# Loading the FFTs' half-way rows: one transfer over 128 partitions, two over 64

## The chip, the cores and the metric

The kernel runs on one core of a Trainium2 chip. The metric is the device time of one execution in microseconds, and lower is better. Before the change, three runs gave 878.99, 880.49 and 887.65 us, a median of 880.49.

A core has TensorE (PE, matrix products; PEld is its loading of weights), VectorE (DVE), ScalarE (ACT), GpSimd (POOL) and SyncE (SP). SP, ACT and POOL can issue DMA transfers, which run on the core's 16 DMA engines. On-chip memory has 128 partitions; DRAM holds inputs, outputs and scratch tensors.

## The reference

One forward pass and its gradients, with L = 2048 positions, D = 448 channels, N = 256 states and F = 1792 hidden units, all in bf16:

```python
g = sigmoid((x * gate_w).sum(-1, keepdims=True))
# branch A: a state-space convolution, computed by FFT
P = exp(dt * A * l)                      # l = 0..2047, rounded to bf16
K = einsum("dn,dnl,dn->dl", C, P, dt * B).real
a = irfft(rfft(pad(u)) * rfft(pad(K)))[:L] + u * Dskip
# branch B: two dense layers with a squared relu
b = relu(x_B @ w1 + b1) ** 2 @ w2 + b2
out = g * a + (1 - g) * b
# returned: out, and the gradients of all inputs but x_B for a given grad_out
```

The gradient of the convolution needs two more products in the frequency domain: one that gives the gradient of K, and one that gives the gradient of u.

## The kernel before

**FFTs in two steps.** A transform of 2048 positions, padded, is done as a product with one small matrix, a trip through DRAM that reorders the rows, and a product with a second small matrix. The forward trips go through the scratch tensors gd[0..2], the inverse ones through hd[0..2]. An inverse transform's first half (inv1_part at L304, or inv1 at L275) writes hd in eight stores of 448 KB, each as 128 x 4 rows of 896 bytes (L315, L291). Its second half reads hd in four quarters q. A quarter is a tile of 128 partitions by 3,584 elements: partitions 0 to 63 take the 64 rows that begin at row 8q of each group of 64 rows in hd, partitions 64 to 127 the rows that begin at 32 + 8q. So a partition receives one contiguous run of 8 x 448 elements, 7,168 bytes, and the two halves differ by a shift of 32 rows. load_hs (L317) does this, with two DMAs on SP's queue.

**Three readers of hd.**
- hd[0] is the convolution that gives the gradient of the taps K. load_taps (L693) issues all four quarters at once into the tile hss, after the last of the eight stores. dk_sums (L701) multiplies them by the Ew matrices on TensorE (L712), copies the sums out on ScalarE (L716), writes them to dk_d (L725) and reads them back as DK (L730).
- hd[1] is the convolution's forward output. A loop over q (L1640) reads one quarter with inv2 (L322, TensorE at L329) and finishes it on VectorE (L1653, L1654). The load for the next quarter is issued while the loop works on this one (L1657).
- hd[2] is the gradient of u. A second loop (L1683) reads one quarter per turn; the first load stands ahead of the loop (L1681), the others one turn ahead (L1686). Its output is copied out at L1697 and stored by four DMAs on SP at L1704.

hd[1] and hd[2] quarters and the spectra that load_sx reads from sp_d (L1556, 896 KB) share a ring of three buffers.

**What sets the order.** Engines execute their instructions in the order of the program. From L562 that order is written out by hand. In the last part, Fl(n) puts n units of other work (the dense layers' weight gradients, L1217 to L1257) between the steps, and Pg(n) puts pieces of the parameters' gradients on VectorE (L1479 to L1526). SP's queue there carries, in program order: the hd stores (L291), sp loads (L1556), hd loads (L320), br loads (L1587, 448 KB), the parameter loads for the last two groups of channels (L1445, L1459, L1460), whose buffer L1674 frees, and the output stores (L1704). POOL's queue carries rows_in (L1212) and stores of outputs. A wait that stands before a DMA on SP holds everything behind it on SP.

**Around the taps.** After the load of the taps SP issues the next rec tile (L629) and w1 (L1170, L1172), which VectorE needs at L786 and TensorE at L995. powers (L580) is a chain between ScalarE (L610, L613) and VectorE (L611, L615) that runs in pieces beside it.

Of the kernel before, what the change touches and what calls it, by code (L numbers as in the profile page):

```python
# [20 lines left out]
L, D, N, F = 2048, 448, 256, 1792  # L21
# [144 lines left out]
class Ker:  # L166
# [148 lines left out]
            queue.dma_start(bass.AP(tensor=hd, offset=4 * q8 * 128 * D, ap=[[D, 128], [128 * D, 4], [1, D]]), st)  # L315

    def load_hs(self, hd, q, hs):  # L317
        for hp in range(2):
            src = bass.AP(tensor=hd, offset=(32 * hp + 8 * q) * D, ap=[[64 * D, 64], [1, 8 * D]])
            self.nc.sync.dma_start(hs[64 * hp:64 * hp + 64].rearrange("p g x d -> p (g x d)"), src)  # L320

    def inv2(self, hs, q, x, hp, ps, more=()):  # L322

# [11 lines left out]
def kernel(ctx, tc, A_u, A_A_re, A_A_im, A_B_re, A_B_im, A_C_re, A_C_im, A_log_dt, A_Dskip,  # L335
# [1286 lines left out]
    Fl(3)  # L1622
    back1(0, 3)
    hsn = load_hs(1, 0)
    Fl(2)
    product(1, 1, sx[1])
# [13 lines left out]
    for q in range(4):  # L1640
# [15 lines left out]
        if q < 3:  # L1656
            hsn = load_hs(1, q + 1)  # L1657
# [21 lines left out]
    obs += [Dw[:, 6144:7680], GU_[:, 10240:11776]]  # L1679
    pgs = (None for dt in range(2, 4) for _ in param_grads(dt))  # L1680
    hsn = load_hs(2, 0)  # L1681
    Fl(8)
    for q in range(4):  # L1683
# [75 lines left out]
```

## Time and profile before

| | |
|---|---|
| median of three runs | 880.49 us |
| the profiled execution | 872.19 us |
| its span, first to last instruction | 870.4 us |
| mean granted TensorE clock | 0.885 |
| busy: PE, DVE, ACT, POOL | 75%, 78%, 66%, 21% of the span |
| DMA packets, bytes | 138,036, 181.16 MB |
| DMA, mean share of the 16 engines, 140 to 190 us | 0.82 |
| the same, 734 to 816 us and 816 to 870 us | 0.81 and 0.56 |
| granted clock, 140 to 190 us and 734 to 816 us | 0.68 and 0.92 |

The profile is of one execution. Times in its views count from the start of the span. A busy engine is not one that sets the end: what does is read from the chain of waits, which goes back from the last instruction, at each step to what released it. A DMA's time in that chain runs from its issue to its landing, when its last byte is known to be in place and the semaphore that readers wait for is full. The shares of the DMA engines are averages over the 16; a stretch in which two of them work all the time and 14 rest shows as 0.125.

The trace also lists each DMA packet (queue, size, start, duration) and each update of a semaphore by a DMA, with its time. The packets do not carry the name of their engine.

### The profile page before, as it was taken

What the parts mean: (1) busy time and instruction counts of PE and PEld (TensorE: products, weight loads), DVE (VectorE), ACT (ScalarE), POOL (GpSimd) and SP (SyncE); (2) the same over time, 40 slices, a digit from 0 to 9 for tenths busy, and PEclk for the clock granted to TensorE, in tenths of its full rate; (3) what the DMA queues carried; (4) which work ended last, traced back from release to release, by engine and by line L of the source; (5) the groups of instructions that cost most, each with busy time, mean ns of one, the idle gap of its engine ahead of it and who ended that gap; (6) DMA issues with size and microseconds to landing.
All of it is one profiled execution on the core that took longest, in us unless ns stands there. A gap on an engine that the chain in (4) does not pass through costs nothing.

```text
span 870.4 us, 19323 instructions
## 1 busy us (share of the span) xinstructions
PE 654.3 (75%) x7849; PEld 344.6 (40%) x7849; DVE 676.5 (78%) x1124; ACT 578.4 (66%) x845; POOL 179.7 (21%) x297
## 2 busy tenths in 40 slices
PE   3857662567688788998978897987847884888496
PEld 2213221342434545554554454455524342444242
DVE  4686998774997888999999989998447965775166
ACT  1896753678787989997858675767734772544262
POOL 1443102141112000000202120214433310123012
PEclk9965797858699889999989987999979997999699
DMA  9968798951555953877456657394889999796872
GB/s 193 265 188 311 232 397 290 251 184 73 156 167 188 229 126 104 189 192 192 133 153 156 206 147 190 97 224 122 202 286 341 290 307 316 247 287 207 237 188 62
DMA packets 138036, 181.16 MB, mean 208 GB/s; under 512 B 67511, under 2 KB 111532, under 8 KB 137420
## 3 DMA queue, kind: packets, MB, share of 16 engines
q1 hardware_dynamic: 116156, 105.94, 45.6%
q0 software_dynamic: 21360, 72.09, 24.9%
q10 hardware_dynamic: 432, 1.90, 1.0%
q8 instruction: 61, 1.00, 0.5%
q14 instruction: 27, 0.22, 0.1%
HBM read 96.97 MB, written 68.97 MB: 191 GB/s over the span
## 4 chain that ended last, share of the span: by engine, by line
PE 31%; ACT 17%; issue 16%; DVE 15%; DMA 14%; POOL 3%; SPq 3%; ACTq 0%; POOLq 0%; DVEq 0%
PE psX L1230 7%; PE psN L1022 4%; PE psN L995 3%; DVE D L665 2%; DVE Y L770 2%; DMA K<-hd 2%; DVE F L771 2%; DMA gd<-R 2%; DMA K<-gd 2%; PE psF L903 1%; PE psF L863 1%; ACT R L865 1%; DVE P L919 1%; DVE Y L773 1%; DMA hd<-st 1%
## 5 line engine op out<-in xcount | busy, mean ns | idle before, releaser
L1022 PE MATMUL psN<-D,S 128*128 128x448 bf16 x448 | 97.0, 365 | 0.0
L773 DVE TENSOR_TENSOR Y<-Y,F 128x256 bf16<-128x256 bf16 (+2 forms) x84 | 72.8, 867 | 2.9
L770 DVE TENSOR_TENSOR Y<-Y,F 128x256 bf16<-128x256 bf16 (+2 forms) x84 | 72.8, 867 | 2.7
L771 DVE TENSOR_TENSOR F<-Y,F 128x256 bf16<-128x256 bf16 (+2 forms) x84 | 71.8, 855 | 0.0
L908 ACT CAST R<-psF 128x1024 bf16<-128x1024 f32 x56 | 57.1, 1019 | 10.2 <-PE psF L903 8.9
L995 PE MATMUL psN<-S,U 128*128 128x512 bf16 x168 | 49.0, 420 | 16.4 <-ACT S L984 11.2
L1230 PEld LDWEIGHTS <-S 128*128 128x128 bf16 x448 | 43.3, 102 | 44.6 <-issue 15.1
L919 DVE TENSOR_TENSOR P<-R 128x2048 bf16<-128x2048 bf16 x42 | 49.4, 1220 | 13.7 <-ACT R L908 13.7
L1022 PEld LDWEIGHTS <-S 128*128 128x128 bf16 x448 | 41.9, 101 | 42.7 <-issue 11.6
L1230 PE MATMUL psX<-D,S 128*128 128x449 bf16 x224 | 51.9, 379 | 1.9 <-ACT S L1237 1.9
L1027 POOL DMA_DIRECT2D br_d<-D x32 | 17.5, 547 | 169.0 <-ACT D L1026 169.0
L822 PE MATMUL psX<-X,Y 128*64 128x16 bf16 x1792 | 39.1, 185 | 15.2 <-DVE Y L773 15.2
L1126 PE MATMUL psN<-S,U 128*128 128x512 bf16 x168 | 44.1, 395 | 5.5 <-ACT S L1135 5.5
L863 PE MATMUL psF<-ident,Y 128*128 128x128 bf16 x448 | 34.4, 238 | 15.8 <-ACT R L865 13.3
L1221 ACT ACTIVATE S<-psN 128x1024 bf16<-128x1024 bf16 x33 | 33.8, 1025 | 18.0 <-PE psN L1217 18.0
L822 PEld LDWEIGHTS <-Y 128*64 128x64 bf16 x1792 | 37.4, 125 | 19.7 <-DVE Y L773 16.5
L865 ACT COPY R<-psF 128x2048 bf16<-128x2048 bf16 x15 | 28.0, 1866 | 22.4 <-PE psF L863 22.4
L759 DVE TENSOR_TENSOR X<-X,F 128x512 bf16<-128x512 bf16 (+1 forms) x70 | 37.5, 536 | 2.6
L1105 POOL DMA_DIRECT2D dhT_d<-S x28 | 20.3, 727 | 89.4 <-DVE S L1102 60.7
L1230 PE MATMUL psX<-U,S 128*128 128x448 bf16 x176 | 37.7, 358 | 1.1 <-ACT S L1234 1.1
L863 PEld LDWEIGHTS <-Y 128*128 128x128 bf16 x448 | 30.2, 107 | 19.5 <-issue 15.7
L760 DVE TENSOR_TENSOR F<-X,F 128x512 bf16<-128x512 bf16 (+1 forms) x70 | 36.9, 528 | 0.0
(330 smaller groups left out, 1660.1 us busy)
## 6 DMA issues: line engine op xcount, KB each, us to landing
hd<-st SPq DMA_DIRECT2D x19, 448.0 KB, 4.0
sp<-K POOLq DMA_DIRECT2D x8, 896.0 KB, 8.6
S<-rT_d SPq DMA_DIRECT2D x16, 448.0 KB, 5.7
dhT_d<-S POOLq DMA_DIRECT2D x28, 256.0 KB, 3.3
S<-rT_d POOLq DMA_DIRECT2D x14, 512.0 KB, 6.4
R<-sp SPq DMA_DIRECT2D x8, 896.0 KB, 10.1
S<-dhT_d POOLq DMA_DIRECT2D x14, 512.0 KB, 5.6
R<-hd SPq DMA_DIRECT2D x16, 448.0 KB, 8.1
```

The lines of the kernel that those rows point to most:

```text
L759: V.tensor_tensor(out=hi4, in0=lo, in1=bcast_dims(pr, [0, (None, n), 1]), op=ALU.mult)
L770: V.tensor_tensor(out=hi, in0=lo, in1=bcast_dims(pr, [0, (None, n // 2), 1]), op=ALU.mult)
L771: V.tensor_tensor(out=Vv.rearrange("p (x a q) -> p x a q", x=rows, q=2), in0=lo, in1=bcast_dims(pi, [0, (None, n // 2), 1]), op=ALU.mult)
L773: return V.tensor_tensor(out=T4[:, :, :, n:2 * n], in0=T4[:, :, :, n:2 * n], in1=V4, op=ALU.add)
L822: T_.matmul(ps[64 * jt:64 * jt + 64, ch * NA:ch * NA + NA], lhsT=Y[:, w, t, :], rhs=XW[:, 1 - t, w, :, 1], start=(k == 0), stop=(k == 3), ...
L863: T_.transpose(pt[:, h, i], Y[:, 16 * g + 8 * h + i].rearrange("p t b -> p (t b)"), ident[:])
L908: S.copy(zb[:, :, :, g % 2].rearrange("p s t n -> p t s n"), psz[:].rearrange("p t (s n) -> p t s n", s=2))
L919: V.tensor_tensor(out=pr.rearrange("p s t g n -> p s t (g n)"), in0=zv, in1=(xb if r == 0 else rev_dim(xb, 2)), op=ALU.mult)
L995: T_.matmul(pss[k][:], lhsT=w1w[:, dt, j * P:j * P + P], rhs=UT[:, dt, 512 * lc:512 * lc + 512], start=(dt == 0), stop=False, skip_group_c ...
L1022: T_.matmul(ps[:, 0:D], lhsT=hb[j][:, P * tt:P * tt + P], rhs=ws[:, j, :], start=(w == 1 and j == 0), stop=(j == FT - 1))
L1126: T_.matmul(pss[k][:], lhsT=w2Tw[:, jp, dt, k], rhs=dblk[:, dt], start=(dt == 0), stop=False, skip_group_check=True)
L1230: T_.matmul(ps[:, 0:w], lhsT=hn[i % 2][th][:, t - 8 * th, :], rhs=(DB2[:, t, :] if i < FT else U[:, t, 0:w]), start=(t == 0), stop=(t == L ...
```

## The change

load_hs issues one DMA per quarter instead of two. The source, in DRAM, is now a pattern of three counts: 2 blocks that are 32 rows apart, 64 rows in each that are 64 rows apart, and one run of 8 x 448 elements. The destination is the whole tile, 128 partitions. The same bytes go to the same places. load_taps calls it four times, the two loops eight times: 24 DMAs become 12.

```diff
     def load_hs(self, hd, q, hs):
-        for hp in range(2):
-            src = bass.AP(tensor=hd, offset=(32 * hp + 8 * q) * D, ap=[[64 * D, 64], [1, 8 * D]])
-            self.nc.sync.dma_start(hs[64 * hp:64 * hp + 64].rearrange("p g x d -> p (g x d)"), src)
+        src = bass.AP(tensor=hd, offset=8 * q * D, ap=[[32 * D, 2], [64 * D, 64], [1, 8 * D]])
+        self.nc.sync.dma_start(hs.rearrange("p g x d -> p (g x d)"), src)
```

An access pattern lists [step, count] pairs, the slowest first.

## The prediction

> **What bounds the kernel now.** I read the page's shares first, then the chain of waits in time order, then the two stretches in which the changed loads run.
>
> The chain by engine (page, part 4):
>
> ```profile
> PE 31%; ACT 17%; issue 16%; DVE 15%; DMA 14%; POOL 3%; SPq 3%; ACTq 0%; POOLq 0%; DVEq 0%
> ```
>
> No engine owns the span, so a late transfer matters only where the chain runs through it. Where that is for hd, the chain in order of time says (start, length, what):
>
> ```profile
> 138.07 9.50 DMA hd<-st
> ...
> 152.57 14.61 DMA K<-hd
> ...
> 816.63 6.47 DMA R<-hd
> ```
>
> And the engines that wait for hd, from TensorE's own rows (start, length; in brackets the idle time before and what ended it):
>
> ```profile
> 163.14 0.36 PE L712 MATMUL psN<-K,M 128*32 128x448 bf16 x1 [2.81 <-DMA K<-hd]
> ...
> 167.22 0.55 PE L712 MATMUL psN<-K,M 128*32 128x448 bf16 x3 [1.40 <-DMA K<-hd]
> ```
> ```profile
> 821.10 0.56 PE L329 MATMUL psN<-R,cb_Etw 64*32 64x448 bf16 x4 [11.01 <-DMA R<-hd]
> ...
> 823.15 0.56 PE L329 MATMUL psN<-R,cb_Etw 64*32 64x448 bf16 x4 [0.62 <-DMA R<-hd]
> ```
>
> So the taps (hd[0], four quarters) are on the path at 167.2 us, and the first hd[2] quarter at 821. The DMA issues (KB each, median us from issue to landing):
>
> ```profile
> R<-sp SPq DMA_DIRECT2D x8, 896.0 KB, 10.1
> R<-hd SPq DMA_DIRECT2D x16, 448.0 KB, 8.1
> K<-hd SPq DMA_DIRECT2D x8, 448.0 KB, 10.6
> dk_d<-st SPq DMA_DIRECT2D x2, 28.0 KB
> ```
>
> 24 loads of 448 KB become 12 of 896 KB. How they spread over the 16 DMA engines I took from the trace's DMA packets. Every row is one packet of 7,168 bytes. In the taps' stretch (148 to 170 us) 512 such packets take a median 529 ns; for K<-gd and R<-sp, which write 128 partitions (659 to 684 us), the median is 272 ns. The smallest of all 5,904 is 269 ns. 512 x 0.513 us (the mean) / 16 = 16.4 us, against 17.3 from the first packet to the last: one engine moves its rows one after the other.
>
> **The change, part by part.** Removed: 12 issues on SP at 0.59 us (median), 7.1 us of SP's time; this counts only where SP is on the chain, 5.3 us at 147.8 for eight issues, of which 2.6 would go. The bytes, waits and destinations stay, and no load moves in the order.
>
> What decides is how many engines one merged load uses. Its DRAM side counts 2 x 64 rows, its tile side 128 partitions. One SP transfer of before has two sides that differ: dk_d<-st of 28 KB (L725) writes 8 x 4 rows of DRAM from 32 partitions. In the trace's semaphore updates each of the two makes 9: one about 1.0 us after issue and 8 at 1.7 to 2.3 us. Transfers whose sides both start with a multiple of 16 (all hd loads of before) make 16; a one-row transfer (L732) makes one early and one late; the last store, 14 rows (L1727), one early and 14 late. The late ones are engines that finish, so L725 ran on 8: the outer count of the DRAM side, not the 32 partitions. By these rows a side that starts with 2 leaves two engines, 64 rows each.
>
> The Trainium skill, "DMA: Bandwidth & Descriptors", § Why a DMA increments its semaphore by 16 and not by 1, says the same: the largest k up to 16 that divides the slowest dimension of both patterns. By it k is 2; the nine updates agree. The same page, § Rules for kernel authors, advises against two half-partition transfers and for one of 128 partitions; by that sentence alone the time would be that of the first rival.
>
> The price of a load on two engines: 64 x 0.272 = 17.4 us at least. The trace shows no such load alone, so the other end is 64 x 0.529 = 33.9. I take 272 ns: the long rows appear with 64- or 32-partition destinations written by 16 engines together, and two engines do not crowd each other like that. Landings in before keep the order of issue (the eight tap loads end 2.1 us apart), so what is issued later waits on these two engines.
>
> *Taps.* First packet at 149.1, four loads in a row 69.6 us, 0.7 to land: 219.4 instead of 167.2, +52.2. Nothing hides it. TensorE has the dk sums next and then kgen (L822); ScalarE copies the sums before it can square for the powers (L610), for which VectorE already waits 5.4 us at 174.98. The 2.6 us of issue lie beside the transfer and save nothing. Behind the taps in the two engines' queue stand rec (8 rows of 3,840 bytes) and w1 (24 rows of 3,584 at 0.145, and 2 x 4 more): about 7 us, so they land near 227. Their readers, VectorE at 183.7 and L995 at 192.4, move to 236 and 245, so these stay covered.
>
> *hd[1], from 734.* The first quarter starts at 735.5; POOL's queue has 12 us of packets per engine in 735 to 792, so I add 2 us a load: it lands at 755, its reader (L329) stood at 744.3, +11. Before the next in the queue come two hd stores (64 rows of 896 bytes at 41 ns, 2.6) and an sp load (8 x 0.272 = 2.2): 755 + 4.8 + 19.4 = 779, reader 760.9 + 11, now +18. Third: 2.6 + 2.2 and a br load 1.1: 804.5, reader 779.2 + 18, now +25. Fourth: 2.6 + 1.1: 827.6, reader 792.3 + 25, now +35.4. The slack of 3.4 to 5 us that each load had is used up in these.
>
> *hd[2].* Its first load waits on SP behind the parameter loads, which wait for the buffer that L1674 frees after the last hd[1] reader, so it goes out at 816 + 35.4 and needs 1.4 + 17.4 + 0.7 = 19.5 where its first half took 5.1: +14.4, now +49.8, at 870.9. The other three follow in the queue: 17.4, then twice 17.4 + 1.5 (four output stores). The last lands at 926, its reader stood at 845.65: +80. The 24.7 us from there to the end stay.
>
> Sum: +52 + 80 = +132. The profiled execution took 872.19 us (span 870.4 and 1.8 around it), so it would take 1,004; the runs' median 880.49 lies 8.3 above it, which gives 1,013 there. I say 1,010.
>
> **Rivals.** *All 16 engines are used*, because the two row counts are merged or split before the engines see them. Then it is faster: the tap rows fall from 529 to 272 ns, 8.7 us of packets instead of 17.3; but VectorE and ScalarE regain only the 5.4 us of VectorE's wait. In the tail the first, third and fourth hd[2] loads (no slack) land some 2 us sooner, 6 together. 872 - 11 = 861, or 869 on the median. For it: the 272 ns rows of the 128-partition loads; against: L725's nine updates. It decides from an outer count of 16 up.
>
> *Two engines, but another pair for each load.* Loads then overlap. Taps: each lands 19.5 us after issue, the last at 170; the four groups of sums then run in one piece of 10 us from 167.3, +7. Tail: +10 at the first hd[1] load, +3 and +5 at the third and fourth, +14 at the first hd[2], +12 and +1 at its third and fourth: 45. Together +52: 925 to 933. The packets carry no engine's name, so nothing excludes it but the even order in which landings come. On HWDGE, the page named above says in that section, it is the lowest-numbered k; by it this rival falls.
>
> *Two engines at 529 ns a row*, if the 57,344-byte step between rows and not the partitions makes the rows long. 12 loads x 16.4 us more: about 1,200. Against it: when the first hd[1] quarter ran alone (734 to 742 us), 14 of its 128 rows took under 300 ns, at the same step.
>
> **How the numbers follow.** Two engines in one queue at about 272 ns: 0.85. All engines: 0.06. Changing pairs: 0.05. Long rows: 0.04. The time is that of the first. Its own range: 768 rows lie in line (12 x 64), so 10 ns a row are 7.7 us; rows of 340 ns beside other traffic give +52, 1,065. Low, 960: if POOL's rows fall between the loads (-8 in the first tail stretch), if the stores and sp loads between them land before they cost (-17), and if the clock, granted at 0.68 in 140 to 190 us and 0.92 in the tail, is given back after longer pauses and TensorE's later work runs some per cent quicker (-20). 960 to 1,065 holds most of the first case, some 0.8 in all; all rivals lie outside it. A change of 1% is about what measurements of this kernel tell apart (three runs spread 879.0 to 887.7). Faster: 0.05, the first rival where it reaches past 1%. Same: 0.02, its rest and a load hidden better than I see. Slower: 0.93.
>
> **What would show it.** Each merged load has an early semaphore update and two late ones, and lands about 19 us after issue, the taps' last some 70 us after the first packet; its rows stay at 272 ns. TensorE's waits before L712 grow from 9 us (four waits) to some 61, ScalarE and VectorE idle with it; L329 shows a wait at nearly every quarter. The mean DMA share in these stretches falls to two engines' worth, near 0.12. I am wrong if the loads land within 8 us, or if the taps land together, near 170 us.

## The result and the profile after

Four runs of the changed kernel gave 1036.43, 1040.88, 1041.48 and 1045.04 us, a median of 1041.18 against 882.64 for the kernel before in the same comparison. The ratio is 1.1789, with a 95% interval of 1.1708 to 1.187: the change costs 158.5 us. The forecast was 1,010. The profiled execution took 1036.43 us, its span is 1034.7. One line is gone from load_hs, so line numbers behind it are one lower than before.

The chain of the changed kernel, first by engine, then by line (page, part 4):

```profile
DMA 14%; PE 5%; SPq 1%; ACT 1%; DVE 1%; issue 0%; POOL 0%; POOLq 0%; ACTq 0%; DVEq 0%
DMA R<-hd 13%; PE psX L1229 2%; SPq L1555 1%; DMA Y<-t_d 1%; PE psN L1711 1%; PE psN L328 0%; DVE K L1673 0%; PE psF L326 0%; PE psN L1247 0%; PE psF L328 0%; ACT S L1236 0%; PE psN L326 0%; SPq L1444 0%; ACT st L219 0%; PE psN L1216 0%
```

The shares do not add up to 100, because the way back was lost at about 800 us: the view seems to look for 16 updates per landing, and a merged load no longer makes 16. The DMA issues of SP's queue have no time to landing any more either (KB each):

```profile
R<-hd SPq DMA_DIRECT2D x8, 896.0 KB
...
K<-hd SPq DMA_DIRECT2D x4, 896.0 KB
```

More than half of what is left of the chain (13 of some 22 points) is in one row: R<-hd, the loads of the two loops. Who waited for whom, longest first (us in total, times, longest):

```profile
PE psN L328 <- DMA R<-hd: 99.6, 8, 27.0
...
DVE F L614 <- ACT P L609: 77.5, 9, 64.6
...
PE psN L711 <- DMA K<-hd: 63.2, 4, 17.7
ACT st L715 <- PE psN L711: 63.0, 2, 43.4
```

TensorE waits for each of the 12 loads, and the taps' wait goes on to ScalarE (the copies of the sums, L715) and from there to VectorE (L614), which had 5.4 us of it before and has 64.6 in one piece now. TensorE's rows at the four taps quarters, and at the eight quarters of the loops (idle time before each in brackets):

```profile
172.08 1.35 PE L711 MATMUL psN<-K,M 128*32 128x448 bf16 x12 [17.69 <-DMA K<-hd]
...
189.52 1.35 PE L711 MATMUL psN<-K,M 128*32 128x448 bf16 x12 [14.23 <-DMA K<-hd]
...
208.91 0.53 PE L711 MATMUL psN<-K,M 128*32 128x448 bf16 x1 [16.18 <-DMA K<-hd]
...
228.09 0.91 PE L711 MATMUL psN<-K,M 128*32 128x448 bf16 x3 [15.06 <-DMA K<-hd]
```
```profile
822.44 0.56 PE L328 MATMUL psN<-R,cb_Etw 64*32 64x448 bf16 x4 [15.05 <-DMA R<-hd]
...
849.35 0.56 PE L328 MATMUL psN<-R,cb_Etw 64*32 64x448 bf16 x4 [8.39 <-DMA R<-hd]
...
878.33 0.56 PE L328 MATMUL psN<-R,cb_Etw 64*32 64x448 bf16 x4 [10.25 <-DMA R<-hd]
...
904.10 0.56 PE L328 MATMUL psN<-R,cb_Etw 64*32 64x448 bf16 x4 [10.18 <-DMA R<-hd]
...
950.86 0.56 PE L328 MATMUL psN<-R,cb_Etw 64*32 64x448 bf16 x4 [26.99 <-DMA R<-hd]
...
968.99 0.56 PE L328 MATMUL psN<-R,cb_Etw 64*32 64x448 bf16 x4 [8.71 <-DMA R<-hd]
...
988.94 0.56 PE L328 MATMUL psN<-R,cb_Etw 64*32 64x448 bf16 x4 [10.43 <-DMA R<-hd]
...
1007.78 0.56 PE L328 MATMUL psN<-R,cb_Etw 64*32 64x448 bf16 x4 [9.54 <-DMA R<-hd]
```

The quarters come 18 to 29 us apart, apart from the long gap before 950.86, in which the parameter loads and the fifth load's 20 us lie. Before, TensorE's waits for hd in the loops were 11.6 us in all, both at the first hd[2] quarter.

How many engines a load uses can be counted in two ways. Each merged load makes three semaphore updates, one about 1 us after issue and two when it lands. And the rows of 7,168 bytes that are in flight at the same moment, from the starts and durations of the packets in the taps' stretch:

| taps' loads of | rows in flight, mean | duration of a row, mean | first to last, us |
|---|---|---|---|
| before | 15.2 | 513 ns | 17.3 |
| after | 2.0 | 293 ns | 74.9 |

Where the time went, from the two profiled executions (1034.7 - 870.4 = 164.3 us of span):

| stretch | before | after | difference |
|---|---|---|---|
| start to the taps' first issue | 147.8 | 151.3 | +3.5 |
| that issue to the first reader of the last taps quarter | 19.4 | 76.8 | +57.4 |
| to the first hd[1] issue | 567.0 | 570.5 | +3.5 |
| to the first reader of the last hd[2] quarter | 111.4 | 209.2 | +97.8 |
| to the end | 24.8 | 26.9 | +2.1 |

So 155 of the 164 us lie in the two stretches in which hd is read.

### The profile page after: what moved, and what is told of

The parts are those of the page before. It is cut to its first block, busy times and chain, and to the rows that moved or that the text cites. A ratio compares the mean times of both kernels' runs of the same rounds, so it can differ in the third digit from the quotient of the medians.

```text
span 1034.7 us, 19274 instructions
## 1 busy us (share of the span) xinstructions
PE 673.6 (65%) x7819; PEld 354.3 (34%) x7849; DVE 676.2 (65%) x1124; ACT 578.6 (56%) x845; POOL 177.0 (17%) x297
## 5 line engine op out<-in xcount | busy, mean ns | idle before, releaser
L1021 PE MATMUL psN<-D,S 128*128 128x448 bf16 x448 | 94.6, 359 | 0.0
L328 PE MATMUL psN<-R,cb_Etw 64*32 64x448 bf16 x64 | 9.0, 549 | 99.6 <-DMA R<-hd 99.6
L1229 PE MATMUL psX<-D,S 128*128 128x449 bf16 x224 | 57.8, 411 | 1.7 <-ACT S L1236 1.7
L614 DVE TENSOR_TENSOR F<-P 128x256 f32<-128x256 f32 (+1 forms) x20 | 7.8, 389 | 77.9 <-ACT P L609 77.5
L994 PE MATMUL psN<-S,U 128*128 128x512 bf16 x155 | 46.7, 423 | 14.9 <-ACT S L983 10.9
L1218 DVE COPY S<-psS 128x1024 bf16<-128x1024 bf16 x14 | 9.6, 687 | 71.5 <-PE psS L1216 71.5
L711 PE MATMUL psN<-K,M 128*32 128x448 bf16 x88 | 12.2, 555 | 63.2 <-DMA K<-hd 63.2
L862 PE MATMUL psF<-ident,Y 128*128 128x128 bf16 x448 | 37.1, 249 | 16.7 <-ACT R L864 13.0
L209 ACT CAST F<-psN 128x448 bf16<-128x448 f32 x18 | 9.8, 546 | 66.8 <-PE psN L328 57.8
L1125 PE MATMUL psN<-S,U 128*128 128x512 bf16 x151 | 42.3, 395 | 6.9 <-ACT S L1134 5.7
L1026 POOL DMA_DIRECT2D br_d<-D x32 | 17.4, 545 | 168.3 <-ACT D L1025 168.3
L328 PEld LDWEIGHTS <-cb_Etw 64*32 64x32 bf16 x128 | 4.0, 93 | 116.9 <-issue 116.9
```

The source lines that it names most:

```text
L862: T_.transpose(pt[:, h, i], Y[:, 16 * g + 8 * h + i].rearrange("p t b -> p (t b)"), ident[:])
L994: T_.matmul(pss[k][:], lhsT=w1w[:, dt, j * P:j * P + P], rhs=UT[:, dt, 512 * lc:512 * lc + 512], start=(dt == 0), stop=False, skip_group_c ...
L1021: T_.matmul(ps[:, 0:D], lhsT=hb[j][:, P * tt:P * tt + P], rhs=ws[:, j, :], start=(w == 1 and j == 0), stop=(j == FT - 1))
L1125: T_.matmul(pss[k][:], lhsT=w2Tw[:, jp, dt, k], rhs=dblk[:, dt], start=(dt == 0), stop=False, skip_group_check=True)
L1229: T_.matmul(ps[:, 0:w], lhsT=hn[i % 2][th][:, t - 8 * th, :], rhs=(DB2[:, t, :] if i < FT else U[:, t, 0:w]), start=(t == 0), stop=(t == L ...
```

## The experiments

Each kernel is compared with runs of the kernel before on the same chip. Its median moved between 875.8 and 883.5 from chip to chip, so the ratios count.

**Taps alone, loops alone.** load_hs got a flag that chooses between the two forms; one kernel sets it in load_taps, the other in the two loops:

```diff
-            K.load_hs(hd[0], q, hss[q])
+            K.load_hs(hd[0], q, hss[q], True)
```
```diff
-        K.load_hs(hd[w], q, hs)
+        K.load_hs(hd[w], q, hs, True)
```

> Only the four taps loads (hd[0]) go as one transfer of 128 partitions each; the eight loads of hd[1] and hd[2] stay as before. Theory (two engines per merged load, the four loads one after the other): the changed kernel's stretch between the taps' issue and their last landing, 76.8 us against 19.4 before, comes alone, so the median lies 57 to 64 us above before, 940 to 947, and each taps load makes three semaphore updates. Rival (pairs of engines that change, loads that overlap): +7, about 890. If the taps were harmless and all cost came from the loops: 883.

> The eight loads of hd[1] and hd[2] are merged, the four taps loads stay as before. Theory: the tail's part alone, 97.8 us at the last reader and 2 after it, so +95 to +103, 978 to 986; with the kernel that merges only the taps the two excesses add up to the changed kernel's 158.5 within 8 us. Rival (the parts are not independent, for instance since the lower granted clock is carried from one to the other): the two excesses add up to 140 or less.

Measured: 943.94 for the taps alone, ratio 1.0731 (1.0669 to 1.0794), and 985.91 for the loops alone, ratio 1.1193 (1.114 to 1.1246), before 881.32. The excesses are 62.6 and 104.6, together 167 against 158.5: 8.7 more, a little above the 8 that was asked; the intervals of the three ratios (about 0.6, 0.5 and 0.8% of 880 us to either side) are wide enough to hold it. Each part costs about what it costs in the whole. In the kernel with merged taps the loops' last reader comes 111.1 us after the first hd[1] issue (before 111.4), in the one with merged loops 209.0 (after 209.2). The parts are independent, and the rival with changing pairs (+7 for the taps) falls.

**One transfer over 128 partitions, with a straight DRAM side.** If partition 2p + half takes the row that partition 64 half + p took, the DRAM side is 128 rows at one step. The matrices Et and Ew have their rows in that order, and as a half is no longer a block of partitions, inv2 multiplies over 128 rows, with a second matrix for the other half, which one more DMA loads:

```diff
-        for hp in range(2):
-            src = bass.AP(tensor=hd, offset=(32 * hp + 8 * q) * D, ap=[[64 * D, 64], [1, 8 * D]])
-            self.nc.sync.dma_start(hs[64 * hp:64 * hp + 64].rearrange("p g x d -> p (g x d)"), src)
+        src = bass.AP(tensor=hd, offset=8 * q * D, ap=[[32 * D, 128], [1, 8 * D]])
+        self.nc.sync.dma_start(hs.rearrange("p g x d -> p (g x d)"), src)
...
-            nc.tensor.matmul(ps[32 * l0g:32 * l0g + 32], lhsT=Et[64 * hp:64 * hp + 64, l0g, 2 * q + x, :],
-                             rhs=hs[64 * hp:64 * hp + 64, l0g, x, :],
+            nc.tensor.matmul(ps[32 * l0g:32 * l0g + 32], lhsT=Et[:, l0g, 2 * q + x, :],
+                             rhs=hs[:, l0g, x, :],
```

> One transfer over 128 partitions whose DRAM side counts 128 rows straight through (partition 2p + half instead of 64 half + p; the second-step matrices have their rows in that order, and the loops' products run over 128 rows, half of them times zero). Theory (the outer count of 2 decides, not the size or the 128 partitions): 16 engines, 16 semaphore updates, rows of about 272 ns, taps landed 8 us sooner than before; 861 to 876, 7 to 20 below before. Rival (one transfer over 128 partitions is slow in itself): about 1040. Rival (the rows stay at about 500 ns at 16 engines because of where they lie in DRAM): 875 to 890, no change.

Measured: 873.60 (10 runs) against 881.32 (19 runs), ratio 0.9915 (0.9873 to 0.9958). 16 updates per load, 15.1 rows in flight in the taps, median row 272 ns. Its DMA issues and two of TensorE's rows in the taps:

```profile
R<-hd SPq DMA_DIRECT2D x8, 896.0 KB, 7.2
K<-hd SPq DMA_DIRECT2D x4, 896.0 KB, 7.3
```
```profile
152.58 1.35 PE L714 MATMUL psN<-K,M 128*32 128x448 bf16 x12 [0.17 <-DMA K<-hd]
...
157.34 0.35 PE L714 MATMUL psN<-K,M 128*32 128x448 bf16 x1 [0.57 <-DMA K<-hd]
```

The same 12 loads of the same size into the same 128 partitions, and TensorE hardly waits for the taps: the dk sums end 14.7 us after the taps' first issue, where they took 22.7. Not all of these 8 us are kept: ScalarE's copies of the sums end 22.0 us after the first issue, 24.6 in the kernel before, and VectorE's wait behind them (5.4 us before) is still 1.4. VectorE copies the next rec tile 33.4 us after the first issue, 36.0 in the kernel before, so 2.6 us are left by then. VectorE's row before, then in this kernel (first issues at 147.8 and 148.1):

```profile
183.73 0.62 DVE L786 COPY X<-rec 128x512 bf16<-128x512 bf16 x1 [2.23 <-PE psX L822]
```
```profile
181.52 0.61 DVE L788 COPY X<-rec 128x512 bf16<-128x512 bf16 x1 [2.23 <-PE psX L824]
```

The loops' stretch keeps its length (110.8). Where the rest of the 7.7 us by the medians lies, the profiles do not show: from that copy to the first hd[1] issue the profiled executions of all these kernels took 550 to 561 us, with no edit in between. So neither the size nor the single issue makes the change slow. This version is 0.9% faster than the kernel before (by its interval 0.4 to 1.3%).

**Two transfers over every second partition.** The same matrices, with before's step in DRAM:

```diff
-            self.nc.sync.dma_start(hs[64 * hp:64 * hp + 64].rearrange("p g x d -> p (g x d)"), src)
+            self.nc.sync.dma_start(hs[hp:128:2].rearrange("p g x d -> p (g x d)"), src)
```

> The same order of rows and the same matrices, but two transfers per quarter as before: each has 64 rows with before's step of 57,344 bytes in DRAM, and goes to every second partition, so that each is spread over all 128. It tells what makes before's rows 500 to 530 ns long. If it is that 16 engines write only 64 neighbouring partitions: rows of about 272 ns, and a time within 5 us of the single interleaved transfer. If it is the step in DRAM: rows of about 520 ns, and before's time within 6 us.

Measured: 873.17, ratio 0.992 (0.9889 to 0.9951), the same as the single transfer. Median row 272 ns (518 to 529 in kernels that load 64 neighbouring partitions with 16 engines). The step in DRAM is that of before, so it is the neighbouring partitions that made before's rows long; the issues that were saved (12 x 0.59 us of SP) are worth nothing that can be measured.

**A DRAM side of three counts with 16 and with 4 outside.** Two transfers of 64 partitions as before, with the rows of each in another order, and Et and Ew to match:

```diff
-            src = bass.AP(tensor=hd, offset=(32 * hp + 8 * q) * D, ap=[[64 * D, 64], [1, 8 * D]])
+            src = bass.AP(tensor=hd, offset=(32 * hp + 8 * q) * D, ap=[[64 * D, 16], [1024 * D, 4], [1, 8 * D]])
```
```diff
+            src = bass.AP(tensor=hd, offset=(32 * hp + 8 * q) * D, ap=[[64 * D, 4], [256 * D, 16], [1, 8 * D]])
```

> Two transfers of 64 partitions per quarter, as before, but the DRAM side of each counts 16 x 4 rows (three counts with the run, as the changed kernel has; the second-step matrices have their rows in that order). Theory (the outer count decides): 16 engines, 16 semaphore updates, rows of about 520 ns, 876 to 888, before's time. Rival (a DRAM side of three counts is slow in itself): each load lands after 10 us or more, 920 or above.

> The same with 4 x 16 rows. Theory: five semaphore updates, one early and four late; 16 rows per engine and transfer at about 272 ns, 8.7 us per quarter, all on the same four engines. Taps: 34.8 us of rows, +17 at the last landing; tail: the hd[1] loads nearly covered (+3), the hd[2] loads +8 to 14. Together 907 to 918. Rival (three counts are slow in themselves): the same time as with 16 x 4 rows. Rival (all engines but another order): 881.

Measured: 878.36 with 16, ratio 1.003 (0.9988 to 1.0071); 946.87 with 4, ratio 1.0848 (1.0782 to 1.0915), before 875.82.

| outer count | semaphore updates | rows in flight | row, mean | ratio |
|---|---|---|---|---|
| 16 | 16, all late | 15.3 | 501 ns | 1.003 |
| 4 | 1 early, 4 late | 3.9 | 351 ns | 1.085 |
| 2 (after) | 1 early, 2 late | 2.0 | 293 ns | 1.179 |

The outer count, up to 16, is the number of engines in every case here, and three counts are not slow in themselves. The cost at 4 was about twice what was expected: +71 against +31 to +42. The rows fall into two groups, near 274 and near 500 ns, so the taps' rows took 46.6 us and not 34.8, and the loops' stretch grew by 34 us. Four engines that write 64 neighbouring partitions seem to hinder one another as 16 do; this was not tried by itself.

**The merged loads on GpSimd's queue.**

```diff
-        self.nc.sync.dma_start(hs.rearrange("p g x d -> p (g x d)"), src)
+        self.nc.gpsimd.dma_start(hs.rearrange("p g x d -> p (g x d)"), src)
```

> The changed kernel with its 12 merged loads issued by GpSimd instead of SP. It asks whether it is the queueing on one and the same pair that costs, or the 17.4 us of each load. If GpSimd's loads take another pair each time: the four taps loads land together some 20 us after issue, +4 to +8 there, and the tail keeps about +45, so 925 to 945. If they stay on one pair: 1020 to 1050, as the changed kernel.

Measured: 1001.11, ratio 1.1417 (1.1357 to 1.1477): neither number. In the taps 5 to 8 rows were in flight for most of the time, the four loads landed together (177.0 to 180.5 us), and the dk sums ended 41.6 us after the first issue, against 82.2 in the changed kernel. So pairs do change there, and queueing on one pair is about two thirds of what the taps cost: 82.2 - 41.6 = 40.6 us of 82.2 - 22.7 = 59.5. That the loads took over 30 us and not the expected 20 goes in part to longer rows, 350 ns in the mean; why these are longer with 8 engines was not tried. The prediction had +7 at the taps for changing pairs; here it is 41.6 - 22.7 = 18.9. In the loops nothing was won (216.8 us to the last reader). GpSimd's own rows show why (start, length, in brackets the idle time before):

```profile
790.65 0.53 POOL L1211 DMA_DIRECT2D S<-dhT_d  x1 [23.96 <-PE psN L1216]
791.17 0.83 POOL L319 DMA_DIRECT2D R<-hd  x1
```

The load of the second hd[1] quarter stands behind rows_in, which waits 24 us for TensorE, which waits for the first quarter. The one turn of lead is lost, and each load's own length (21 to 35 us) shows in full.

**Without GpSimd's rows in the last part.** In both kernels the 14 loads of dhT_d are left out, so the weight-gradient products that use them run on older data:

```diff
-        if i < NU:
+        if i < FT:
             G_.dma_start(hr[i % 3], bass.AP(tensor=(rT_d if i < FT else dhT_d), offset=(i % FT) * P * L, ap=[[L, P], [1, L]]))
```

> The changed kernel without the 14 loads of dhT_d on GpSimd's queue in the last part (the products that use them run on older data). It asks for the size of a term: GpSimd's rows between the merged loads were put at 8 us in the first loop, and the trace after has 19 to 24 us of them per engine there. If that is where the excess over the forecast went: 12 to 22 us faster than the changed kernel, 1019 to 1029, and the first loop's fourth reader comes 12 to 20 us sooner. If the rows of two engines are long for another reason: within 6 us of 1041. The same edit on the kernel before is to follow as a control.

> The control to the kernel without the 14 loads of dhT_d: the same edit on the kernel before (the products that use them run on older data). If GpSimd's rows cost mainly because they share two engines with the merged loads, this one gains little, 0 to 5 us (872 to 882), and the changed kernel's gain of about 16 us by the same edit is theirs. If it gains 12 us or more, the rows cost as much in any queue and explain nothing of the excess.

Measured: the changed kernel falls to 1017.79, ratio 1.1623 (1.1558 to 1.1688), the kernel before to 873.64, ratio 0.988 (0.9831 to 0.9929). By the ratios the edit is worth 14.6 us to the one and 10.6 to the other (of 880), and the intervals are wider than what is between: by time the control decides nothing. By the profiled stretches it does more: the first loop's fourth reader comes 11.4 us sooner in the changed kernel (94.1 us after the first issue, 105.5 with the rows) and 1.8 in the one before (56.2, 58.0); the whole stretch is 13.6 shorter in the one and 2.5 in the other. In the kernel before and in four others whose loads of the loops use 16 engines (taps alone merged, both interleaved ones, outer count 16) this stretch took 110.0 to 111.4 us, so single profiles do tell such differences apart here. About 11 us of the merged loads' excess are then these rows. The expectation had put them at 19 to 24 us per engine in the first loop; the trace after has 16.4 us of GpSimd's packets per engine from the first issue to the fourth reader, as a mean over the 16.

## Why the prediction was right

The forecast was 1,010 us and 1,041 was measured, in the upper part of its range of 960 to 1,065. For the profiled execution the sum gave 1,004, and it took 1,036: 32 us more, of which 5 are in the taps, 18 in the tail and 9 outside both. The mechanism was right; two terms were too small.

**Two engines per merged load, on one pair, from the DRAM side's outer count: right.** The nine updates of one transfer in the trace of before had shown it, and every run with the loads on SP's queue agrees: 2 rows in flight, 4 with an outer count of 4, 15 with 16 or 128. The rival that all engines are used describes the interleaved kernel instead: with the outer count of 128 its forecast (861 in the profiled execution, 8 tap rows of 272 ns per engine and load) came to a gain of 7.7 us in the median where 11 was said. The 6 us that it saw in the tail did not come, and of the 5.4 us of VectorE's wait 4.0 did (5.36 to 1.36).

**17.4 us per load: nearly right.** In the loops' second half, where little else moved, the rows' median and mean were 274 and 280 ns. Of the two ends (272 and 529) the lower was the right one, and for the reason given: the kernel with two interleaved transfers has 272 ns rows from the same step in DRAM.

**Taps +52: measured +57.4.** The term that was too small is the row: 293 ns in the mean, not 272. 256 rows per engine x 21 ns are 5.4 us.

**Tail +80: measured +97.8.** Up to the fourth reader of the first loop the sum had +35.4, and +47.5 was measured. The term most at fault is that of GpSimd's packets between the loads, 2 us a load. After, one cycle between two landings (849.3 to 878.3 us) took 29.0 us where the sum had 25.3: the load, the hd stores and the sp and br loads at the sizes said or somewhat over, and of GpSimd some 5.5 us of packets per engine. The sum had counted 8 us in all, where the four turns of before had 12 us per engine and those of after had 16.4: more of these packets fall into the longer loop (951 of 4,096 bytes, 837 before), and each takes longer (210 ns, 184 before). The rows are longer too: the fourth load, which ran from 880.0 to 903.6 us, had 298 ns in the mean, which is 1.7 us more for its 64 rows per engine than the sum had. The first hd[2] load was put at +14.4 over the readers before it and came to +17.9. The last three at 18.1, 19.9 and 18.9 us apart stand beside 17.4, 18.9 and 18.9.

**"The clock is given back after longer pauses": it was not.** The prediction's lower end counted up to 20 us for it. The stretches with the waits had a lower granted clock (third figure from the right), not a higher one:

```profile
152.00:228.00 76.00, 11.79 (x117) 5.88 (x115) 18.65 (x33) 12.53 (x18) 0.00 (x0) 0.52 0.23 77
228.00:260.00 32.00, 21.35 (x289) 13.81 (x290) 17.78 (x36) 21.26 (x32) 12.60 (x16) 0.66 0.42 138
260.00:690.00 430.00, 363.08 (x5672) 209.98 (x5700) 375.49 (x556) 337.30 (x444) 67.97 (x113) 0.92 0.62 162
...
798.00:905.00 107.00, 51.96 (x346) 23.69 (x345) 41.78 (x75) 27.24 (x55) 11.15 (x20) 0.76 0.46 149
905.00:1008.00 103.00, 44.59 (x289) 21.22 (x288) 33.89 (x78) 21.09 (x47) 8.40 (x15) 0.72 0.31 104
```

For these three stretches (the first line and the last two) it was 0.74, 0.91 and 0.88 before. What follows the taps' wait got nothing back: 0.66 and 0.92 in the second and third line, 0.68 and 0.92 before (167 to 199 and 199 to 626 us). The mean over the span fell from 0.885 to 0.815. That the lower clock cost little, because TensorE waits there anyway, is an argument and not shown. The Trainium skill, "TensorE: Matmul & The Clock Gate", § Part 1: The HAM clock gate, says that a monitor sets the clock by how busy TensorE has been lately, half of it being the idle state; the trace agrees, with 0.52 in the 76 us in which TensorE waited most.

**The DMA share near 0.12: not as said.** The second figure from the right of the same lines is 0.23 in the taps, 0.46 and 0.31 in the loops. In the taps the rows of 7,168 bytes alone make 0.12, so the merged loads do occupy two engines' worth; the rest is other transfers in the same time, which the forecast left out.

**Slack, and who waits: right.** The slack of 3 to 5 us in the first loop was used up at the first load, rec and w1 stayed covered, and the wait went from TensorE over ScalarE to VectorE as said. Not foreseen was that SP itself stops: the third and fourth taps loads took 16.1 and 17.1 us to issue, and rec and w1 went out only at 186 and 203 us. Each of these stalls is about as long as one load's rows (64 x 0.274 = 17.5 us), as if the queue took the next load only when an earlier one was through; no run shows this directly.

The remaining 9 us of the span's growth lie outside the two stretches. The part from the dk sums' end to the first hd[1] issue, which no edit touches, took 563 to 575 us in the profiled executions of all these kernels, so from one profile of each kernel these 9 us cannot be explained.

## What to carry to other kernels

Before two transfers are made one, look at the slowest count of both sides: merging two blocks puts a 2 there, and here a 2 meant two engines of 16, about 18 us of rows for 896 KB, with everything later on that queue held up behind it. The semaphore updates or the rows in flight show the number of engines at once. If the merge is wanted, change the order of the rows so that the DRAM side has one long outer count; here that gained 0.9%, and two transfers that are each spread over all partitions gained as much, so the gain is not that of the issues saved.

## What was not expected of the hardware

- The granted clock of TensorE falls where TensorE waits: 0.52 in the 76 us of the taps, and the first two groups of four of inv2's products behind a wait for hd take 0.56 us each, in both kernels, where most others take 0.37.
- SP stalls at issue when about two merged loads are outstanding on the pair: 0.6, 0.5, 16.1 and 17.1 us for four issues in a row.
- A 64-row transfer into every second partition has rows of 272 ns, and one into 64 neighbouring partitions 518 to 529 ns, from the same rows of DRAM.
- With an outer count of 2, SP's loads all used one pair (they landed one after the other), and GpSimd's four loads used different ones (5 to 8 rows in flight).
